# Pinning ScalarE's first operation for the w_in pieces only in an attention + FFN + MoE kernel

## The chip, the cores and the metric

One NeuronCore of a Trainium2 chip runs the whole program in one launch. The metric is the device time of that launch in microseconds, as the median of several runs; lower is better. The profile is one further execution with the hardware profiler on.

## The reference, cut to what matters

```python
def reference(q, k, v, M_prev, z_prev, beta, moe_w_in, moe_w_out, w_gate, w1, w2):
    # attention: 4 batches x 8 heads, 576 tokens, 64 wide, causal softmax plus a gated memory read
    x = (g * mem_out + (1 - g) * local)            # -> [2304, 512]
    # dense feed-forward: 512 -> 2048 -> 512
    h = x @ w_in
    x = np.maximum(h, 0.0) ** 2 @ w_out
    # mixture: 8 experts of capacity 288, tokens dealt out in order of their logits
    return moe2(x, w_gate, w1, w2)                 # [2304, 512], float32
```

`w_in` and `w_out` arrive as 64-bit floats and are narrowed to 32 bits on the chip; what else matters here is float32. The change touches how these two weights are made ready.

## The kernel before, in words

**Stages.** The program runs attention for 16 pairs of heads, then the dense feed-forward in three passes over the 2048 hidden columns, then the mixture. The stages overlap: while attention runs, the first pass of the feed-forward (hidden chunks 0 to 5 of 16, `PASSES[0]`) is already prepared and, from the fifth head pair on, computed between attention's matmuls. A step of attention (`step(n)`, n from -2 to 16) works on three or four head pairs at once; its ten sub-steps follow `PLAN` and call `fill` 20 times with a count of feed-forward matmuls that may go in there.

**Weight pieces.** Matmuls run on pairs of a rounded high part and a remainder, so each weight is split first. A piece is 128 partitions by 512 values of 64 bits. The first pass has twelve: pieces 0 to 5 are chunks of `w_in` (part 0), pieces 6 to 11 chunks of `w_out` (part 1). The generator `apart` makes them in this order, and `fill` advances it by one piece at places given in `CONVERT`: two per step in steps 0 to 5 (at the 10th and 20th call of `fill`; in step 5 at the 4th and 10th). So the w_out pieces belong to steps 3, 4 and 5. One piece costs:

- `fetch` (L424): one DMA of 512 KB from SyncE's queue into tile `raw`. There are two such tiles in turn, and the fetch stands in the program one piece ahead of its use. SyncE's queue is in order, and the fetch of piece n+2 waits until piece n has been read by L39.
- `narrow`: L36 on ScalarE (`r<-raw`), then L37, L38 and L39 on VectorE (`gf<-r`, `r<-r,gf`, `gf<-raw,r`).
- `split`: L25 on ScalarE (`win<-gf` or `wout<-gf`) and L26 on GpSimd (`wout<-gf,wout`).

**What sets the order.** TensorE's order is the program's, written by hand (`INORDER`). For the other engines the build plays the program on its own model of times and gives each engine's queue the order that comes out; on the chip each queue then runs strictly in that order, and an instruction whose input is late holds up all behind it. `keep_in_program_order(a)` ties an instruction to come behind the instruction that precedes it on its engine in the program. In `weights` it ties L36 of every first-pass piece (`first` is true when the pool is `f.start`), in `fetch` the DMA of every first-pass piece. For pieces 6, 8 and 11 the preceding ScalarE instruction is the eviction L316 of the first-range read (`read(n, 0, ..)`); for pieces 7 and 9 it is the end of a step; for piece 10 it is the exponential L173 of `phi`. The 20 pieces of the two later passes (`chunks`, pools `cv`) have no such tie.

**Names used below.** L217 scores, L228 and L236 their masking on VectorE, L240 exponentials on ScalarE, L246 scaling on GpSimd, L271 and L287 transposes on TensorE, L25/L26 the high part and remainder of any split, L312 the read of the values, L316 its eviction, L162 the remainder of the values (`vt`), L172 to L185 `phi` (tile `e` has one buffer: L172 of one head pair waits for L180 of the pair before), L474 the sum of two halves of a token block (`xf`), L487 the ReLU that empties the hidden accumulator `ph`.

Of the kernel before, what the change touches and what calls it, by code (L numbers as in the profile page):

```python
# [22 lines left out]
def split(nc, hi, lo, src, eng=None):  # L23

    a = nc.scalar.activation(hi, src, AF.Copy)  # L25
    (eng or nc.vector).tensor_tensor(lo, src, hi.bitcast(F32), op=OP.subtract)  # L26
    return a.ins


def narrow(nc, f, tmp, raw):  # L30

    low, high = raw[..., 0], raw[..., 1]
    a = nc.scalar.activation(tmp.bitcast(F32), high.bitcast(F32), AF.Copy, scale=2.0 ** -112)  # L36
    nc.vector.tensor_scalar(f, tmp, 3, None, op0=OP.logical_shift_left)  # L37
    nc.vector.scalar_tensor_tensor(tmp, tmp, -2 ** 31, f, op0=OP.bitwise_and, op1=OP.bitwise_or)  # L38
    nc.vector.scalar_tensor_tensor(f, low, 29, tmp, op0=OP.logical_shift_right, op1=OP.bitwise_or)  # L39
    return a  # L40
# [353 lines left out]
class Ffn:  # L394
# [34 lines left out]
    def weights(self, c, part, home, pool, eng, psum=None, raw=None):  # L429

        nc = self.nc
        if part == 0:
            a = self.win[c] = home.tile([128, 2, KD, 128], F32R, name="win")
            dst = a.rearrange("p s k f -> p s (k f)")
        else:
            dst = self.wout[c] = home.tile([128, 2, DM], F32R, name="wout")
        first = pool is self.start
        raw = self.fetch(c, part, pool) if raw is None else raw
        t_ = (psum or self.two).tile([128, DM], I32, name="pr" if psum and psum is self.p2x else "r")
        held = part and c >= PASSES[-1][0]  # L440
        f_ = (self.two if first else self.keep if held else pool).tile([128, DM], I32, name="gf")
        a = narrow(nc, f_, t_, raw.rearrange("p (n t) -> p n t", t=2))
        if first:
            self.tc.keep_in_program_order(a)
        split(nc, dst[:, 0], dst[:, 1], f_.bitcast(F32), eng)
        if held:
            self.sums += [(f_, c - PASSES[-1][0], e) for e in range(8)]
        yield
# [846 lines left out]
```

## Time and profile before

| what | before |
|---|---|
| median of 3 runs | 1045.69 us (1044.23 to 1046.37) |
| the profiled execution | 1049.03 us, its span 1047.3 us |
| TensorE busy | 959.4 us (92%) |
| VectorE, ScalarE, GpSimd busy | 655.2, 552.6, 540.3 us |

How to read it: the profiled execution lies 3.34 us above the median of the runs, and its span 1.73 us below its own time. Engines are PE (TensorE), PEld (its weight loads), DVE (VectorE), ACT (ScalarE), POOL (GpSimd) and SP (SyncE); a "q" behind the name is the engine's sequencer. "Idle before" is the time that an engine stood ahead of an instruction, with what ended it.

### The profile page before, as it was taken

To read this page: it belongs to the slowest core of one execution; us is meant where nothing else is said; L and a number is where in the kernel's file an instruction comes from. 1 tells how busy PE (TensorE), PEld (TensorE's weight loads), DVE (VectorE), ACT (ScalarE), POOL (GpSimd) and SP (SyncE) were. 2 spreads that over 40 slices of the span, in tenths; PEclk is the share of its full clock that TensorE was granted. 3 is DMA by queue.
4 is the path that set the end of the run, shared out by engine and by line. 5 is a ranking of instruction groups with operands and counts; after the bars stand their busy time and mean duration, and the time that the engine had idled before them with its cause. 6 is when DMAs were issued, how large, how long until landed. Compare 5 with 4: busy or idle time off the path is not lost.

```text
span 1047.3 us, 19732 instructions
## 1 busy us (share of the span) xinstructions
PE 959.4 (92%) x7017; PEld 879.1 (84%) x7017; DVE 655.2 (63%) x1925; ACT 552.6 (53%) x1370; POOL 540.3 (52%) x535
## 2 busy tenths in 40 slices
PE   5777879999999988999999999999598999999996
PEld 3666668988889987999999999877498888989996
DVE  6889888888888737256427943335775567674110
ACT  6778878888888735444322343431252453344531
POOL 4666776766666525344312121211394865687841
PEclk9778889999999999999999999999698999999999
DMA  6345736374526277769583332101542444437400
GB/s 154 106 123 142 192 89 179 75 196 100 172 67 175 56 233 227 220 223 315 185 293 122 117 125 83 68 12 41 193 162 79 152 184 151 156 130 258 147 28 27
DMA packets 150724, 150.75 MB, mean 144 GB/s; under 512 B 71641, under 2 KB 122841, under 8 KB 150497
## 3 DMA queue, kind: packets, MB, share of 16 engines
q1 hardware_dynamic: 147552, 140.05, 43.6%
q0 software_dynamic: 3072, 9.44, 2.9%
q8 instruction: 55, 0.90, 0.4%
q14 instruction: 45, 0.36, 0.1%
HBM read 111.69 MB, written 37.77 MB: 143 GB/s over the span
## 4 chain that ended last, share of the span: by engine, by line
PE 61%; DVE 12%; issue 7%; DMA 6%; ACT 6%; POOL 5%; SPq 1%; POOLq 0%; DVEq 0%; ACTq 0%
PE ph L1066 12%; PE ph L45 6%; PE ph L46 6%; PE ph L47 6%; PE py L45 4%; PE py L46 4%; PE py L47 4%; PE ps L312 3%; POOL wsp L1050 3%; PE ps L217 3%; PE ps L271 2%; PE rs L843 2%; DMA raw<-in_moe_w_out_dram 1%; DMA raw<-in_moe_w_in_dram 1%; ACT P L240 1%
## 5 line engine op out<-in xcount | busy, mean ns | idle before, releaser
L489 POOL TENSOR_TENSOR gf<-r 128x384 f32<-128x384 f32 (+1 forms) x108 | 87.4, 810 | 206.9 <-ACT r L487 198.1
L1050 POOL TENSOR_TENSOR wsp<-wraw,wsp 128x1024 fp32r<-128x1024 f32 x64 | 150.9, 2393 | 42.8 <-ACT wsp L1048 31.6
L26 DVE TENSOR_TENSOR gs<-gf,gs 128x384 fp32r<-128x384 f32 (+1 forms) x108 | 65.6, 607 | 91.4 <-ACT gs L25 90.9
L1066 PE MATMUL ph<-xs,wsp 128*128 128x288 f32 x768 | 120.0, 306 | 0.0
L1066 PE MATMUL ph<-hs,wsp 128*128 128x288 f32 x768 | 117.5, 307 | 0.0
L246 POOL TENSOR_SCALAR P<-P,R,og 128x128 f32<-128x128 f32 (+2 forms) x144 | 99.5, 707 | 24.6 <-DVE R L244 17.7
L1066 PEld LDWEIGHTS ph<-xs,wsp 128*128 128x128 f32 x768 | 106.6, 192 | 3.6 <-issue 2.8
L1066 PEld LDWEIGHTS ph<-hs,wsp 128*128 128x128 f32 x768 | 107.2, 194 | 0.9 <-DVE hs L1090 0.4
L1048 ACT ACTIVATE wsp<-wraw 128x1024 fp32r<-128x1024 f32 x64 | 64.0, 1051 | 48.6 <-DMA wraw<-in_moe_w_dram 29.1
L487 ACT ACTIVATE r<-ph 128x384 f32<-128x384 f32 (+1 forms) x108 | 48.6, 450 | 77.6 <-PE ph L47 76.5
L240 ACT ACTIVATE P<-P,R 128x128 f32<-128x128 f32 (+2 forms) x144 | 83.4, 580 | 8.4 <-DVE R L228 6.9
L25 ACT ACTIVATE gs<-gf 128x384 fp32r<-128x384 f32 (+1 forms) x108 | 52.5, 486 | 58.0 <-POOL gf L489 49.6
L45 PE MATMUL ph<-xt,win 128*128 128x384 f32 x240 | 81.3, 339 | 0.0
L46 PE MATMUL ph<-xt,win 128*128 128x384 f32 x240 | 80.8, 337 | 0.0
L47 PE MATMUL ph<-xt,win 128*128 128x384 f32 x240 | 80.7, 336 | 0.0
L45 PE MATMUL ph<-xs,win 128*128 128x288 f32 x192 | 64.3, 335 | 10.6 <-ACT r L487 7.6
L271 PE MATMUL ps<-ident,P 128*128 128x128 f32 x320 | 62.3, 302 | 8.6 <-DVE R L228 3.3
L46 PE MATMUL py<-gs,wout 128*128 128x384 f32 x192 | 64.7, 338 | 0.3 <-DVE gs L26 0.3
L47 PE MATMUL py<-gs,wout 128*128 128x384 f32 x192 | 63.9, 336 | 0.0
L26 DVE TENSOR_TENSOR ptb<-ps,ptb 128x384 fp32r<-128x384 f32 (+3 forms) x128 | 59.1, 464 | 7.4 <-ACT ptb L25 5.8
L45 PE MATMUL py<-gs,wout 128*128 128x384 f32 x192 | 63.4, 338 | 0.0
L228 DVE CUSTOM_DVE_ANT_0 P<-ps,maskw 128x128 f32<-128x128 f32 (+3 forms) x128 | 58.5, 483 | 6.2 <-PE ps L217 3.2
(259 smaller groups left out, 2596.4 us busy)
## 6 DMA issues: line engine op xcount, KB each, us to landing
wraw<-in_moe_w_dram SPq DMA_DIRECT2D x32, 1024.0 KB, 5.5
xt<-xs_d SPq DMA_DIRECT2D x12, 1536.0 KB, 7.2
x_d<-xo SPq DMA_DIRECT2D x32, 288.0 KB, 3.8
xf<-x_d SPq DMA_DIRECT2D x32, 288.0 KB, 3.8
xs_d<-xs SPq DMA_DIRECT2D x8, 1152.0 KB, 6.6
raw<-in_moe_w_in_dram SPq DMA_DIRECT2D x16, 512.0 KB, 5.4
raw<-in_moe_w_out_dram SPq DMA_DIRECT2D x16, 512.0 KB, 5.5
yp<-yo SPq DMA_DIRECT2D x32, 144.0 KB, 3.9
```

The lines of the kernel that those rows point to most:

```text
L26: (eng or nc.vector).tensor_tensor(lo, src, hi.bitcast(F32), op=OP.subtract)
L45: nc.tensor.matmul(out, lhi, rhi, start=start, stop=False)
L46: nc.tensor.matmul(out, lhi, rlo, start=False, stop=False)
L47: nc.tensor.matmul(out, llo, rhi, start=False, stop=stop)
L228: nc.vector.tensor_tensor_reduce(out=pw, in0=ps[:, 0:W[u]], in1=maskw[:, 512 - 128 * t:640], op0=OP.add, op1=OP.min, scale=-0.125, scalar= ...
L240: nc.scalar.activation(pw, pw, AF.Exp, bias=R[:, 0, u:u + 1], scale=-1.0, accum_out=R[:, 1, u:u + 1])
L246: nc.gpsimd.tensor_scalar(PP[n][w], PP[n][w], R[:, 2, w:w + 1], og9[:, hp, w:w + 1], op0=OP.mult, op1=OP.mult)
L271: nc.tensor.transpose(tr[:, 128 * i:128 * i + 128], P[:, 128 * i:128 * i + 128], ident)
L489: nc.gpsimd.tensor_tensor(gf, r, r, op=OP.mult)
L1048: nc.scalar.activation(w[:, 0, hs], raw[:, hs], AF.Copy)
L1050: eng.tensor_tensor(w[:, 1, hs], raw[:, hs], w[:, 0, hs].bitcast(F32), op=OP.subtract)
L1066: nc.tensor.matmul(out, l[a], r[b], start=i + p == 0, stop=i == n - 1 and p == 2)
```

## The change

In `weights`, L36 is tied to its place only for pieces with `part` 0, those of `w_in`. For the six pieces of `w_out` the tie is gone, and the build places L36 on ScalarE as it places any other instruction. The tie of the fetches, the places in `CONVERT`, the tiles, and all instructions and their number stay.

```diff
         a = narrow(nc, f_, t_, raw.rearrange("p (n t) -> p n t", t=2))
-        if first:
+        if first and not part:
             self.tc.keep_in_program_order(a)
         split(nc, dst[:, 0], dst[:, 1], f_.bitcast(F32), eng)
```

## Rows read from the trace of the kernel before

**Rows 1.** The page: the span.

```profile
span 1047.3 us, 19732 instructions
```

**Rows 2.** Stretches: us, busy (count) of PE, PEld, DVE, ACT, POOL; clock, DMA, GB/s.

```profile
75.50:96.20 20.70, 16.54 (x101) 13.20 (x100) 20.26 (x60) 17.55 (x52) 13.85 (x15) 0.83 0.58 151
96.20:118.30 22.10, 16.79 (x102) 13.32 (x101) 20.55 (x58) 17.73 (x53) 16.21 (x20) 0.81 0.60 159
118.30:139.00 20.70, 17.98 (x122) 14.73 (x121) 17.30 (x52) 16.41 (x50) 17.04 (x21) 0.94 0.55 149
139.00:148.40 9.40, 3.42 (x17) 3.41 (x18) 6.55 (x15) 5.57 (x12) 7.62 (x10) 0.64 0.63 158
...
191.00:350.00 159.00, 156.57 (x1188) 140.99 (x1187) 133.72 (x405) 134.88 (x410) 104.70 (x136) 1.00 0.48 126
```

**Rows 3.** Line L36, whole span: min/median/max ns, first and last start; idle before.

```profile
L36 ACT ACTIVATE r<-raw x20: 624/660/685, 30.1 to 417.9; 128x512 f32<-128x512 f32 x20
L36 ACT ACTIVATE pr<-raw x12: 607/638/652, 448.0 to 501.4; 128x512 f32<-128x512 f32 x12
...
  DMA raw<-in_moe_w_in_dram: 11.7, 7
  DMA raw<-in_moe_w_out_dram: 7.6, 6
```

**Rows 4.** Line L36, 0 to 160 us (no idle time before it there).

```profile
L36 ACT ACTIVATE r<-raw x12: 645/662/685, 30.1 to 149.2; 128x512 f32<-128x512 f32 x12
```

**Rows 5.** ScalarE in order: start, us, line, operation, [idle before <-what ended it].

```profile
96.24 0.39 ACT L316 ACTIVATE xo<-ps 128x256 f32<-128x256 f32 x1 [1.17 <-PE ps L312]
...
118.30 0.39 ACT L316 ACTIVATE xo<-ps 128x256 f32<-128x256 f32 x1 [1.92 <-PE ps L312]
118.58 0.66 ACT L36 ACTIVATE r<-raw 128x512 f32<-128x512 f32 x1
...
142.44 0.74 ACT L172 ACTIVATE e<-nq 128x640 f32<-128x640 f32 x1 [2.24 <-DVE nr L180]
...
143.84 0.65 ACT L36 ACTIVATE r<-raw 128x512 f32<-128x512 f32 x1
144.51 0.41 ACT L487 ACTIVATE r<-ph 128x288 f32<-128x288 f32 x1
```

**Rows 6.** VectorE in order, around three of the six pieces.

```profile
97.21 0.86 DVE L37 TENSOR_SCALAR gf<-r 128x512 int32<-128x512 int32 x1 [0.62 <-ACT r L36]
...
119.27 0.84 DVE L37 TENSOR_SCALAR gf<-r 128x512 int32<-128x512 int32 x1 [1.36 <-ACT r L36]
...
130.74 0.79 DVE L37 TENSOR_SCALAR gf<-r 128x512 int32<-128x512 int32 x1
131.44 0.40 DVE L26 TENSOR_TENSOR ptb<-ps,ptb 128x256 fp32r<-128x256 f32 x1
```

**Rows 7.** TensorE in order: a wait in step 4, one in step 5, the first use of w_out.

```profile
131.90 0.55 PE L217 MATMUL ps<-kt,qt 64*128 64x128 f32 x6 [1.01 <-DVE ptb L26]
...
144.98 0.61 PE L45 MATMUL ph<-xs,win 128*128 128x288 f32 x1 [6.65 <-ACT r L487]
...
157.75 0.38 PE L45 MATMUL ph<-gs,wout 128*128 128x288 f32 x1
```

**Rows 8.** Lines L37, L38, L39 from 96 to 155 us, the six w_out pieces.

```profile
L37 DVE TENSOR_SCALAR gf<-r x6: 387/606/858, 97.2 to 150.1; 128x512 int32<-128x512 int32 x6
...
L38 DVE SCALAR_TENSOR_TENSOR r<-r,gf x6: 674/693/1279, 99.4 to 150.9; 128x512 int32<-128x512 int32 x6
...
L39 DVE SCALAR_TENSOR_TENSOR gf<-raw,r x6: 677/788/1112, 102.6 to 152.8; 128x512 int32<-128x512 int32 x6
```

**Rows 9.** Fetches: SyncE's issue for piece 8; landing of the six w_out fetches.

```profile
103.57 0.35 SPq L424 DMA_DIRECT2D raw<-in_moe_w_out_dram  x1
...
DMA to landing us min/median/max: 3.7/4.0/6.3
```

**Rows 10.** GpSimd beside the longest L38, that of piece 8, issued at 120.50.

```profile
120.43 0.80 POOL L474 TENSOR_TENSOR xf<-xf 128x288 f32<-128x288 f32 x1 [0.24 <-DMA xf<-x_d]
```

## The prediction, made before the changed kernel was run

> **What bounds the kernel now.** I read the table of stretches first. From 191 to 350 us TensorE is busy 156.57 of 159 us at full clock [rows 2]: there it is the bound, its order is fixed by hand and its work is not touched. What the change can give or take must come before that, in steps 3 to 5 of attention, where the six w_out pieces are made. Step 3 has VectorE busy 20.26 of 20.70 us and 20.55 of 22.10 us in the two stretches that hold it; in step 4 it is at 17.30 of 20.70; between 139.0 and 148.4 us nothing is busy for long, TensorE 3.42 of 9.40 us at a clock of 0.64 [rows 2]. So the bound moves: VectorE first, then a chain of waits, then TensorE. A microsecond won before about 148 us arrives at the end nearly whole, since TensorE is full from there on.
>
> Second, the lists of instructions in order of time, around each L36. ScalarE stands 1.17 and 1.92 us ahead of the eviction L316 and then runs L316 and L36 back to back: 118.30 plus 0.39, next 118.58 [rows 5]. The tie binds, then: L36 goes at the first moment that it may. Third, who waited for it: VectorE stood 0.62 us (piece 6) and 1.36 us (piece 8) until L36 was done [rows 6]. In step 4 TensorE stood 1.01 us for a remainder (L26) that was queued behind piece 9's L37 [rows 6, 7]. In step 5 TensorE stood 6.65 us for the ReLU L487, which started at 144.51 us right behind piece 10's L36 at 143.84 [rows 5, 7].
>
> **The change part by part.** No instruction is added or dropped. What moves is six L36 and, behind them, six each of L37, L38, L39, L25 and the GpSimd L26. They can only go earlier, as the tie was a lower bound. How much earlier is set by the data: piece 8's fetch is issued at 103.57 us and such a fetch lands 3.7 to 6.3 us later, 4.0 in the median [rows 9], so its L36 could go from about 107.6 us, 11 us ahead of 118.58 [rows 5]. The fetches stay tied on SyncE, but each waits for L39 two pieces before, so an earlier L39 lets a fetch go earlier too; that is no cost, since SyncE holds less behind it.
>
> Piece 6. If L36 sits in the 1.17 us ahead of L316 [rows 5], L37 can use the 0.62 us that VectorE stood [rows 6]: a gain of 0.62 us, at most the 0.86 us of L37 itself. VectorE is full on both sides [rows 2], so what it gains counts.
>
> Piece 8. Likewise 1.36 us [rows 6], with room for L36 in 1.92 us [rows 5]. Bounds: nothing, if the operations land in VectorE's full stretch before; up to 2.78 us, the sum of L36 (0.66), L37 (0.84) and L38 (1.28, the longest of its row), if all three leave the path [rows 5, 6, 8]. I take 1.36, the row that shows an engine standing.
>
> Piece 9. L37 (0.79 us) stands ahead of the L26 for which TensorE waits 1.01 us [rows 6, 7]. Gain 0.79, between nothing and 1.01.
>
> Piece 10. L36 leaves the queue between L173 and L487: 144.51 minus 143.84, 0.67 us off the wait of 6.65 [rows 5, 7].
>
> Pieces 7 and 11: nothing. No wait of an engine is shown behind their L36 in steps 3 and 5, and the first use of any w_out tile is at 157.75 us [rows 7]; the last piece's L39 starts at 152.8 at the latest [rows 8].
>
> Sum of gains: 0.62 + 1.36 + 0.79 + 0.67 = 3.44 us.
>
> Costs. Every freed L36 takes 0.66 us of ScalarE at its new place [rows 4]. For pieces 6, 8 and 10 a gap that could take it is in the rows, 1.17, 1.92 and 2.24 us [rows 5]; for piece 9 I know none, and charge 0.66 us. Bounds: 0 and four times 0.66, 2.6 us. GpSimd's subtraction moves with its piece; GpSimd is busy 16.21 and 17.04 us of steps of 22.1 and 20.7 [rows 2], and I charge nothing: if that cover is gone, a due operation of the read waits behind it.
>
> Expected gain: 3.44 - 0.66 = 2.78 us. On the profiled span of 1047.3 [rows 1] that gives 1044.5; its execution lies 3.34 us above the median of the runs, so I take the gain off the median: 1045.69 - 2.78 = **1042.9 us**.
>
> **A rule against it.** Piece 8's L38 took 1.28 us where the shortest took 0.674, and it was issued at 120.50 while a GpSimd addition ran from 120.43 for 0.80 us [rows 8, 10]: it ended 0.55 us after that addition did. The Trainium skill (page "SBUF — State Buffer", section "Who interferes with whom") says that a VectorE operation with two inputs in SBUF and a GpSimd operation that reads SBUF exclude each other, the second waiting until the first is done. The row agrees with it. So where the 18 moved operations land beside GpSimd decides their length. Now they take about 6 x (0.606 + 0.693 + 0.788) = 12.5 us by their medians; at the shortest it is 10.4, at the longest 6 x (0.858 + 1.279 + 1.112) = 19.5 [rows 8]. That is -2.1 to +7.0 us of VectorE work, and it is a rival below.
>
> **The rivals.**
>
> 1. *Slower: ScalarE parks at a freed L36.* The order is made on a model of times; on the chip the fetch may land later than the model has it, and all of ScalarE's queue then stands. The kernel shows it: of the 20 pieces of the later passes, which have no tie, 13 had ScalarE standing for the fetch, 19.3 us in all, 1.48 each [rows 3]; of the twelve tied ones none [rows 4]. At that rate 3.9 of 6 park, 5.8 us. The gains of pieces 6 and 8 are lost with it, those of 9 and 10 (1.46) stay: +4.3 us, **1050.0**. It decides from three parked pieces on (3 x 1.48 is more than 3.44). For it: without the tie L36 may go as soon as the model has the fetch landed, and the model need not be right by 4 us [rows 9]. Against it: ScalarE is busy 17.6 of 20.7 us here [rows 2], the freed operation comes last among those ready, and the fetch stands one piece ahead. 0.22.
>
> 2. *Nothing: VectorE is full.* The moved operations only push others in a stretch that is already 93 to 98% busy [rows 2], and the idle times come back elsewhere. Then 0.7 us at most remains, from piece 10: **1045.3**. 0.22.
>
> 3. *The stall in step 5 goes.* L487 waits behind L172, which waits 2.24 us for L180 [rows 5]. If the new order has L487 ahead of L172, or brings L180 forward by what pieces 8 to 10 leave on VectorE, up to 6.65 - 0.67 = 6.0 us more go: **1036.9**, or about 1040 for half. The order of the two is set by the model and not by the tie, so this is a by-product. 0.10.
>
> 4. *Slower by the port:* the moved operations meet GpSimd's long run of L246 at their longest, +7.0 - 2.78: **1049.9**. Six of six at the longest is unlikely. 0.05.
>
> 5. *It doesn't do what it says:* something else (the fetch, a tile) keeps each L36 where it is: **1045.7**. The leads of about 11 us speak against it. 0.03.
>
> **How the numbers follow.** The forecast itself has 0.38, with a range of its own of 1041.5 to 1044.5. What a measurement of this kernel can tell from no change is about 0.2%, 2.1 us. Faster by more: 0.32 of the forecast's 0.38 and rival 3, 0.42. Within: the other 0.06 less a little, rivals 2 and 5, 0.30. Slower by more: rivals 1 and 4, and the unnamed small part, 0.28. The range leaves out the far half of rival 3 and about half of rivals 1 and 4: 1038 to 1050.
>
> **What would show it.** Right: in the trace after, L36 of pieces 6 and 8 ahead of L316, in its idle time; no idle time of VectorE that ends with L36; L26 ahead of piece 9's L37 and a shorter wait of L217; L487 right behind L173; the stretch 191 to 350 unchanged but about 2.8 us earlier. Wrong: idle time of ScalarE ahead of L36 that a fetch ends (rival 1), the steps as long as before with VectorE's idle time elsewhere (rival 2), a wait of TensorE in step 5 far from 6 us (rival 3), L37 to L39 all near 0.9 to 1.3 us (rival 4). A wait of several microseconds at a new place, where a queue in order meets an operation that the model had earlier, would make the whole sum wrong.

## The result: slower by half a per cent to one per cent

| | before | after |
|---|---|---|
| median | 1046.37 us (1044.23 to 1049.26, 5 runs) | 1052.84 us (1051.41 to 1053.47, 5 runs) |
| ratio after to before | | 1.0053, 95% interval 1.0032 to 1.0074 |
| the same on a second chip | 1055.81 us (17 runs) | 1066.11 us (6 runs), ratio 1.0098, 1.0064 to 1.0132 |
| profiled execution, its span | 1049.03, 1047.3 us | 1051.83, 1050.1 us |

The forecast was 1042.9 us, faster. The time lies outside its range and on the other side.

To compare traces I cut them at the same instructions. TensorE's order is the same in both kernels, so the first transposes L131 of `nk` of successive head pairs (start 73.46, 93.35, 114.66 and, three marks on, 190.54 us before) bound three stretches of the same TensorE work: the **first** stretch (piece 6 lands in it when freed), the **second** (from about 93 us) and the **third** (three head pairs, with the 6.65 us wait for L487). From there on both kernels do the same.

The kernel before was profiled a second time beside the experiments. Here are its stretches two and three (the third in two rows), then those of the changed kernel. Columns are as in [rows 2].

```profile
94.52:115.98 21.46, 16.57 (x100) 12.99 (x100) 20.21 (x58) 18.09 (x54) 15.51 (x18) 0.83 0.60 156
115.98:148.67 32.69, 23.09 (x142) 19.53 (x143) 26.80 (x72) 22.53 (x62) 27.35 (x32) 0.81 0.64 172
148.67:194.00 45.33, 43.63 (x319) 39.20 (x319) 36.55 (x104) 36.21 (x110) 25.91 (x33) 0.95 0.48 126
```

```profile
93.40:123.40 30.00, 23.67 (x100) 18.70 (x100) 21.97 (x58) 18.68 (x53) 20.27 (x22) 0.55 0.49 127
123.40:145.70 22.30, 20.60 (x142) 17.79 (x143) 20.98 (x59) 18.29 (x54) 14.43 (x19) 0.92 0.53 136
145.70:197.00 51.30, 45.40 (x320) 40.03 (x318) 39.41 (x115) 39.27 (x116) 32.78 (x41) 0.93 0.53 140
197.00:356.00 159.00, 156.64 (x1188) 141.13 (x1187) 133.47 (x405) 134.58 (x408) 104.97 (x137) 1.00 0.48 126
```

The second stretch grew from 21.5 to 30.0 us. The same 100 matmuls were busy 23.67 instead of 16.57 us at a granted clock of 0.55 instead of 0.83. GpSimd did 22 operations instead of 18. The third stretch shrank from 78.0 to 73.7 us. Behind it the row of 159 us is that of [rows 2], 156.64 us busy against 156.57. So most of the loss is the second stretch, less a part of it won back in the third; the first is 1 to 3 us longer (table below).

What happens at its start, in the changed kernel: ScalarE's four L36 (pieces 6, 7, 8, and 11), then VectorE, GpSimd and TensorE in order of time (start, us, operation, idle before).

```profile
86.08 0.69 ACT L36 ACTIVATE r<-raw 128x512 f32<-128x512 f32 x1
92.11 0.73 ACT L36 ACTIVATE r<-raw 128x512 f32<-128x512 f32 x1
96.27 0.67 ACT L36 ACTIVATE r<-raw 128x512 f32<-128x512 f32 x1 [0.83 <-DMA raw<-in_moe_w_out_dram]
...
150.31 0.69 ACT L36 ACTIVATE r<-raw 128x512 f32<-128x512 f32 x1 [1.77 <-DMA raw<-in_moe_w_out_dram]
```

```profile
95.81 1.75 DVE L37 TENSOR_SCALAR gf<-r 128x512 int32<-128x512 int32 x1 [1.37 <-POOL win L26]
97.60 0.69 DVE L200 TENSOR_TENSOR qpt<-ps,qpt 64x512 fp32r<-64x512 f32 x1
...
115.35 0.29 DVE L228 CUSTOM_DVE_ANT_0 P<-ps,maskw 128x128 f32<-128x128 f32 x1 [1.71 <-PE ps L217]
...
120.58 0.42 DVE L228 CUSTOM_DVE_ANT_0 P<-ps,maskw 128x256 f32<-128x256 f32 x1 [3.93 <-PE ps L135]
```

```profile
94.51 1.27 POOL L26 TENSOR_TENSOR win<-gf,win 128x512 fp32r<-128x512 f32 x1
95.74 1.54 POOL L177 TENSOR_TENSOR e<-qp,zb 128x640 f32<-128x640 f32 x1
```

```profile
98.34 1.33 PE L217 MATMUL ps<-kt,qt 64*128 64x384 f32 x6 [1.96 <-DVE qpt L200]
...
101.92 2.52 PE L217 MATMUL ps<-kt,qt 64*128 64x512 f32 x6
...
115.68 2.17 PE L312 MATMUL ps<-ptb,vt 128*128 128x320 f32 x8
...
190.07 0.39 PE L304 MATMUL ps<-qpt,mb 128*128 128x320 f32 x1 [2.46 <-DVE ptb L26]
```

Pieces 6, 7 and 8, which stood 11 us apart, now come within 10 us. Piece 7's L37 writes one of two tiles `gf`; piece 5's subtraction on GpSimd (94.51 plus 1.27) still reads the one it needs, so L37 waits 1.37 us. It then takes 1.75 us, where the longest of before took 0.86 [rows 8], beside L177 on GpSimd. L200, whose end frees the PSUM bank that the scores L217 write, is queued behind it, and TensorE stands 1.96 us. The same two instructions in the second profile of the kernel before:

```profile
101.13 1.29 PE L217 MATMUL ps<-kt,qt 64*128 64x512 f32 x6
...
109.69 1.25 PE L312 MATMUL ps<-ptb,vt 128*128 128x320 f32 x8
```

Behind the wait the changed kernel's matmuls take nearly twice as long up to about 120 us: 2.52 against 1.29, 2.17 against 1.25. There the roles turn: VectorE stands 1.71 and 3.93 us for L217 and L135; before, its waits for TensorE in this stretch come to 0.2 us.

### The profile page after: what moved, and what is told of

Same layout as the page of the kernel before. It is cut to its first block, busy times and chain, and to the rows that moved or that the text cites. A ratio compares the mean times of both kernels' runs of the same rounds, so it can differ in the third digit from the quotient of the medians.

```text
span 1050.1 us, 19731 instructions
## 1 busy us (share of the span) xinstructions
PE 967.3 (92%) x7017; PEld 885.2 (84%) x7017; DVE 654.7 (62%) x1925; ACT 553.8 (53%) x1370; POOL 540.7 (51%) x535
## 4 chain that ended last, share of the span: by engine, by line
PE 63%; DVE 11%; issue 7%; DMA 6%; POOL 5%; ACT 5%; SPq 2%; POOLq 0%; DVEq 0%; ACTq 0%
PE ph L1066 12%; PE ph L45 7%; PE ph L46 6%; PE ph L47 6%; PE py L45 4%; PE py L46 4%; PE py L47 4%; PE ps L312 3%; PE ps L217 3%; POOL wsp L1050 3%; PE rs L843 2%; PE ps L271 2%; DMA xf<-x_d 2%; PE ps L131 1%; DVE ptb L26 1%
## 5 line engine op out<-in xcount | busy, mean ns | idle before, releaser
L26 DVE TENSOR_TENSOR gs<-gf,gs 128x384 fp32r<-128x384 f32 (+1 forms) x108 | 67.4, 624 | 92.7 <-ACT gs L25 92.3
L487 ACT ACTIVATE r<-ph 128x384 f32<-128x384 f32 (+1 forms) x108 | 48.6, 450 | 78.0 <-PE ph L47 76.8
L45 PE MATMUL ph<-xt,win 128*128 128x384 f32 x240 | 81.4, 339 | 0.0
L45 PE MATMUL ph<-xs,win 128*128 128x288 f32 x192 | 64.1, 334 | 3.8 <-ACT yo L526 2.5
L26 DVE TENSOR_TENSOR ptb<-ps,ptb 64x64 fp32r<-64x64 f32 (+3 forms) x128 | 59.1, 463 | 8.0 <-ACT ptb L25 6.4
L45 PE MATMUL py<-gs,wout 128*128 128x384 f32 x192 | 63.4, 338 | 0.0
```

The costliest lines, as they stand in the source:

```text
L45: nc.tensor.matmul(out, lhi, rhi, start=start, stop=False)
```

## The experiments

All kernels of a set ran on one chip, beside the kernel before on that chip. The edits are to the kernel before, where nothing else is said; c counts from 0 for piece 6 to 5 for piece 11. One table for all; lengths of the three stretches in us, from one profile each, and the second's granted clock where I read it:

| kernel | L36 free | first | second (clock) | third | ratio, 95% interval |
|---|---|---|---|---|---|
| before | none | 19.9 | 21.3 (0.82) | 75.9 | |
| before_again | none | 19.9 | 21.5 (0.83) | 78.0 | 1.0004, 0.9977 to 1.0031 |
| after | 6 to 11 | 22.8 | 30.0 (0.55) | 73.7 | 1.0053, 1.0032 to 1.0074 |
| after_again | 6 to 11 | 21.0 | 30.4 (0.56) | 73.1 | 1.0098, 1.0064 to 1.0132 |
| free678 | 6, 7, 8 | 22.3 | 29.7 (0.62) | 72.9 | 1.0067, 1.0036 to 1.0098 |
| free6_7 | 6, 7 | 20.9 | 26.7 (0.69) | 74.9 | 1.0050, 1.0022 to 1.0078 |
| free6 | 6 | 20.9 | 20.0 (0.84) | 76.7 | 1.0020, 0.9994 to 1.0046 |
| free7 | 7 | 19.9 | 22.4 | 77.0 | 1.0025, 1.0003 to 1.0047 |
| free8 | 8 | 22.4 | 22.5 | 77.1 | 1.0039, 1.0015 to 1.0062 |
| free9_11 | 9, 10, 11 | 20.5 | 20.6 | 73.0 | 0.9953, 0.9927 to 0.9980 |
| free10 | 10 | 19.9 | 20.7 (0.92) | 72.9 | 0.9943, 0.9918 to 0.9968 |
| free10_again | 10 | 19.9 | 21.7 (0.84) | 73.0 | 0.9978, 0.9956 to 1.0000 |
| not7 | all but 7 | 21.2 | 21.8 (0.81) | 77.8 | 1.0043, 1.0019 to 1.0067 |
| not6 | all but 6 | 19.9 | 24.6 (0.79) | 74.4 | 1.0034, 1.0007 to 1.0061 |
| slow200 | none | 19.9 | 26.9 (0.83) | 76.9 | 1.0083, 1.0055 to 1.0110 |
| after_busy | 6 to 11 | 20.9 | 25.8 (0.68) | 71.5 | 1.0015, 0.9989 to 1.0041 |
| before_busy | none | 19.9 | 21.4 (0.84) | 78.0 | 1.0006, 0.9984 to 1.0029 |
| free10_busy | 10 | 19.9 | 23.1 (0.85) | 75.3 | 0.9990, 0.9966 to 1.0014 |
| after_gw | 6 to 11 | 20.9 | 26.9 (0.63) | 75.0 | 1.0018, 0.9995 to 1.0040 |
| before_gw | none | 19.9 | 20.7 (0.92) | 77.2 | 1.0049, 1.0030 to 1.0067 |

Two profiles of one kernel (before, after, free10) agree within 1.0 us in the second stretch and 2.1 in the third. In the first, single profiles are off by 2 us: the 22.4 of free8 lie ahead of anything that its edit moves. Behind the third stretch, where all kernels do the same, the profiled executions last 851 to 867 us, up to 7 us apart on one chip. So a profile's total shows none of these effects; the ratios are of medians.

**Halves of the change.** The first question was which pieces carry the loss.

```diff
-        if first:
+        if first and not (part and c < 3):      # free678
+        if first and not (part and c > 2):      # free9_11
+        if first and not (part and c == 4):     # free10
```

> Only pieces 6, 7 and 8 lose the tie, 9 to 11 keep it. In the changed kernel these three run their L36 at 86.1, 92.1 and 96.3 us, all within step 3. Theory A (three pieces crowd VectorE's queue in step 3, where it is full; L37 of piece 7 stands for a gf buffer and the clock falls behind it): the step that holds 93 to 123 us stays near 30 us as against 21.3 before, and since piece 10 keeps its tie the wait of TensorE for L487 in step 5 stays too, so 5 to 10 us over the kernel before. Theory B (ScalarE parks at L36 for its fetch): 0.83 us of parking is all there is in these three, so at most 1 us slower.

> Only pieces 9, 10 and 11 lose the tie, 6 to 8 keep it. Theory A: steps 3 is as in the kernel before, the 6.65 us wait of TensorE for L487 in step 5 goes or shrinks below 2 us, so 3 to 7 us faster than the kernel before. Theory B: parking at L36 of piece 11 (1.77 us in the changed kernel) makes it 0 to 2 us slower. Theory C (what hurts is the step after, 146 to 174 us, 28.5 us in the changed kernel as against 21.2 before, and pieces 9 to 11 cause it): 3 to 7 us slower.

> Only piece 10 loses the tie. Theory A: the wait of TensorE for L487 in step 5 (6.65 us before) goes or falls below 2 us because L487 no longer stands behind L172, L173 and L36; 3 to 6 us faster than the kernel before. If the wait is made by L172 alone: 0.7 us faster, the wait about 6 us.

Pieces 6 to 8 alone give the loss, 1.0067, with the long second stretch. Pieces 9 to 11, and 10 alone, make the kernel faster: the wait of L45 for L487 is gone from the list of TensorE's waits in the third stretch of free10, which now begins (line, waited for: us in all, times, longest):

```profile
PE ps L312 <- POOL vt L162: 1.7, 1, 1.7
PE ps L131 <- issue: 1.5, 1, 1.5
PE ps L271 <- POOL gf L489: 1.4, 1, 1.4
```

On ScalarE L487 now stands ahead of L172, where it stood behind it [rows 5]:

```profile
140.53 0.41 ACT L487 ACTIVATE r<-ph 128x288 f32<-128x288 f32 x1
...
144.98 0.73 ACT L172 ACTIVATE e<-nq 128x640 f32<-128x640 f32 x1
```

Of the 6.65 us that wait cost, that stretch became 3.0 to 5.1 us shorter (72.9 against 75.9 and 78.0); the time gained is 2.3 us (0.22% on one chip) to 6.0 us (0.57% on another). free678 shows the other side of it: its wait for L487 is 7.43 us, longer than before, and its third stretch is 72.9 us too, so this wait and the length of the stretch don't go one to one.

**Which of 6, 7 and 8.**

```diff
+        if first and not (part and c == 0):     # free6 (free7: c == 1, free8: c == 2)
+        if first and not (part and c < 2):      # free6_7
```

> The tie is taken from L36 of piece 6 alone. Theory A (crowding: the loss needs piece 7 close behind piece 6 in step 3, where its L37 waits for one of two gf tiles and L200 stands behind it): L36 of piece 6 starts at about 86 us as in the changed kernel, piece 7 stays near 107 us, TensorE doesn't wait about 2 us for L200 near 98 us, the step behind it stays near 21 us, and the ratio to the kernel before is within 0.998 to 1.002. Rival B (the loss comes from piece 6 being early at all, because its three VectorE operations land in a full stretch): the step is 25 us or longer and the ratio is 1.003 or more.

> The tie is taken from L36 of piece 7 alone; piece 6 stays behind L316 at about 96 us and piece 7 goes right behind it. Theory A: nothing is crowded into 86 to 97 us, so the step from 93 us keeps its 21 us; pieces 6 and 7 now share the time from 97 to 105 us, and the second L37 waits for a gf tile there, at most about 1.5 us: ratio 0.998 to 1.004. Rival B (each freed early piece costs about a third of the 0.67% of the three together): 1.002.

> The tie is taken from L36 of piece 8 alone; it goes right behind piece 7 at the end of step 3, so that VectorE's idle 1.36 us ahead of its L37 can go, as the prediction had it. Theory A: 0.996 to 1.000, a gain of up to 1.4 us, the step from 93 us unchanged. Rival B: 1.002.

> The ties of pieces 6 and 7 are taken. Theory A: the crowding is back with these two: L36 at about 86 and 92 us, L37 of piece 7 waits more than 1 us for GpSimd's subtraction, TensorE waits about 2 us for L200 near 98 us at a granted clock well below 0.8 in the step from 93 us, which takes 26 to 30 us; ratio 1.003 to 1.008, nearly all of the loss of the three together. Rival B: two thirds of 0.67%, 1.0045, but without the wait for gf. Rival C (it takes all three, since the fetch of piece 8 and its parking are needed): 0.998 to 1.002.

The second stretch bears out theory A: it is 20.0 to 22.5 us with one piece free and 26.7 with 6 and 7, where VectorE's and TensorE's rows repeat those of the changed kernel:

```profile
98.67 1.74 DVE L37 TENSOR_SCALAR gf<-r 128x512 int32<-128x512 int32 x1 [2.20 <-POOL win L26]
100.45 0.69 DVE L200 TENSOR_TENSOR qpt<-ps,qpt 64x512 fp32r<-64x512 f32 x1
```

```profile
101.19 1.33 PE L217 MATMUL ps<-kt,qt 64*128 64x384 f32 x6 [1.96 <-DVE qpt L200]
```

No idle time of ScalarE ahead of an L36 ends with a fetch in free6_7, so the loss needs no parking. But the times don't bear theory A out alone: the single pieces cost 0.20, 0.25 and 0.39%, which for 7 and 8 is what rival B had, though their second stretch is not long. The interval of piece 6 includes 1 and that of piece 7 begins at 1.0003; for piece 8 a loss is left that I can't place. Its profile can't show it: that execution took 1046.68 us, the shortest of its twelve, with a median of 1051.23. Rival B is not excluded.

**One tie put back.** Both start from the changed kernel.

```diff
-        if first and not part:
+        if first and (not part or c == 1):      # not7 (not6: c == 0)
```

> The changed kernel with the tie put back for piece 7 alone; 6 and 8 to 11 stay free. If the crowding of pieces 6 and 7 on VectorE and its two gf tiles is the cause: piece 7 at about 107 us or later, no wait of L217 for L200 near 98 us, the step from 93 us at 20 to 23 us with a granted clock of 0.8 or more, and with the gain of pieces 9 to 11 kept, a ratio of 0.992 to 0.998. If the loss belongs to any early piece: 1.002 or more.

> The changed kernel with the tie put back for piece 6 alone; 7 to 11 stay free. Pieces 6 and 7 now stand back to back behind L316, at about 97 us. If the crowding has to meet the L200 of the second head (at 95 to 98 us) to hurt: no such wait, the step at 21 to 24 us, ratio 0.994 to 1.000. If two early pieces in this step are enough wherever they stand: step 26 us or more, ratio 1.003 or more.

With piece 7 tied the second stretch is 21.8 us again and L217 doesn't wait for L200: both have to be early for that. With piece 6 tied it is 24.6, between my two expectations. But the ratios stay above 1, against what theory A expected: in not7 the third stretch is 77.8 us, so the gain of pieces 9 to 11 isn't there. The crowding of 6 and 7 accounts for the long second stretch and not for all of the time; what not7 and not6 lose stays open. In the third stretch GpSimd's L474 waits longer for its load (`xf`) than before; first not7, then the changed kernel (123.4 to 197 us), then before_again:

```profile
POOL xf L474 <- DMA xf<-x_d: 8.7, 2, 6.7
```

```profile
POOL xf L474 <- DMA xf<-x_d: 17.8, 4, 7.6
```

```profile
POOL xf L474 <- DMA xf<-x_d: 4.5, 2, 4.3
```

In the changed kernel the longest of them ends at 188.34, and TensorE's longest wait of the stretch, 2.46 us at 190.07, comes behind it, though what ended that wait was VectorE's L26. The load was issued at 184.76, behind loads of q and k and stores in SyncE's queue, where before_again has the fourth such load ahead of them (171.53). One of those, and the load:

```profile
182.35 1.05 SPq L78 DMA_DIRECT2D nk<-in_k_dram  x2
...
184.76 0.60 SPq L473 DMA_DIRECT2D xf<-x_d  x1
```

How much of the third stretch this costs was not measured by itself.

**The wait and the clock.** The 30 us hold a wait of 2 us and matmuls that are 7.1 us longer. Is the clock the price, or the held queue? slow200 adds VectorE work to the kernel before; after_busy and before_busy repeat three transposes ahead of the waiting L217, into the same place, so that TensorE works there instead of standing.

```diff
-                nc.vector.tensor_tensor(q_[o, c0:c1], src, q_[a, c0:c1].bitcast(F32), op=OP.subtract)
+                [nc.vector.tensor_tensor(q_[o, c0:c1], src, q_[a, c0:c1].bitcast(F32), op=OP.subtract) for _ in range(5 if n == 3 and part == 0 and j == 1 else 1)]
```

```diff
-                for i in range(t + 1):
+                for i in [i for _ in range(3 if n == 3 and step == 5 else 1) for i in range(t + 1)]:
                     nc.tensor.transpose(tr[:, 128 * i:128 * i + 128], P[:, 128 * i:128 * i + 128], ident)
```

> The kernel before with all ties, and the disputed cost alone: the subtraction L200 of the second head of pair 3 (at 95.0 us in the trace of the kernel before, 0.69 us) is issued five times instead of once, with the same inputs and result, so that the scores L217 behind it (at 96.79 us) wait about 2 us, as they do in the changed kernel. Theory A1 (a stall of this size in step 3 lets the granted clock fall, and the longer matmuls are most of the loss): the granted clock of the step from 93 us goes from 0.82 to 0.65 or less, the step goes from 21.3 us to 26 us or more, ratio 1.003 to 1.006. Rival A2 (a stall costs what it lasts; the loss comes from the three pieces' work itself): the step takes 23 to 24.5 us, clock about 0.8, ratio 1.001 to 1.0025.

> The changed kernel with the three transposes L271 that stand ahead of the waiting scores L217 (at 95.5 us) issued three times, into the same place, so that TensorE works in the 1.96 us in which it stood. If the granted clock that follows the wait is most of the loss: clock of the step at 0.75 or more, L217 of 64x512 near 1.0 us instead of 2.52, step of 24 us or less instead of 30, ratio 0.998 to 1.003. If the held VectorE queue is the loss by itself: step of 27 us or more whatever the clock, ratio 1.005 to 1.010.

> The kernel before, all ties in place, with the three transposes L271 ahead of L217 (at 96.0 us there) issued three times. TensorE doesn't wait at that place in this kernel. If what helped the changed kernel was the filled wait: no gain here, step from 93 us 21 to 23.5 us (six transposes of 0.15 to 0.3 us each in a step that VectorE fills), ratio 0.999 to 1.003. If six more transposes there help in any case: 0.997 or less.

> The kernel with the tie taken from piece 10 alone, which gave 0.9943 and 0.9978, with the same six transposes. If the filled wait is what matters: no further gain, 0.995 to 1.000. If the transposes help in any case: below 0.994.

slow200 fits neither theory: its length is A1's, its mean clock A2's, and its time lies above both. The build spread the five L200 from 95.57 to 107.77 us, so the scores didn't wait; another matmul did, for the last of them. The stretch took 26.9 us with TensorE's busy time and mean clock unchanged:

```profile
93.90:120.80 26.90, 16.70 (x100) 13.53 (x101) 22.87 (x62) 18.80 (x52) 18.55 (x22) 0.83 0.50 136
```

```profile
108.52 0.58 PE L304 MATMUL ps<-qpt,mb 128*128 128x256 f32 x1 [2.84 <-DVE qpt L200]
```

So 4 x 0.69 = 2.8 us of VectorE work in this stretch cost 5.4 us of it (26.9 against 21.5), and 8.8 us of the kernel (0.83%), with no longer matmuls in sum. In this run the added work cost twice its length in the stretch; that other work does so is not shown. The other 3.4 us are not explained.

The equal mean hides that the low level of the clock moved. Here are parts of the second stretch in before_again, slow200, the changed kernel and after_busy; the granted clock is the third number from the end, 0.50 is 1.2 GHz and 1.00 is 2.4 GHz:

```profile
96.00:101.00 5.00, 4.74 (x21) 3.77 (x21) 4.32 (x11) 2.06 (x5) 3.23 (x4) 0.50 0.79 185
102.00:113.00 11.00, 9.03 (x64) 7.14 (x60) 10.56 (x36) 10.88 (x35) 7.82 (x10) 1.00 0.39 105
```

```profile
98.00:104.00 6.00, 3.44 (x21) 2.08 (x19) 5.84 (x13) 4.25 (x9) 0.84 (x3) 1.00 0.58 141
106.00:111.00 5.00, 2.48 (x11) 2.48 (x12) 3.94 (x15) 3.23 (x10) 2.91 (x3) 0.50 0.54 164
112.00:118.00 6.00, 4.25 (x36) 3.54 (x34) 3.75 (x11) 3.97 (x13) 6.00 (x7) 1.00 0.28 90
```

```profile
94.00:98.00 4.00, 2.38 (x11) 1.76 (x9) 2.60 (x3) 2.70 (x6) 4.00 (x4) 0.50 1.07 263
98.00:119.00 21.00, 18.10 (x71) 14.44 (x72) 16.08 (x46) 11.70 (x36) 12.91 (x17) 0.50 0.36 96
```

```profile
94.00:110.00 16.00, 13.38 (x54) 10.61 (x54) 13.58 (x30) 9.11 (x22) 11.54 (x13) 0.50 0.64 151
112.00:119.00 7.00, 5.35 (x42) 4.35 (x40) 4.99 (x20) 6.83 (x26) 5.66 (x8) 1.00 0.51 130
```

In slow200 the low level lies about its wait of 2.84 us and not ahead of it, and is about as long as before. In the changed kernel the clock was low already when the wait of 1.96 us began (96.38), as it was at this place in before_again. What differs is that it stayed low until about 120 us, across that wait and four shorter ones (0.26 to 0.99 us). In free678 the clock was high through a wait of 2.26 us at this place and low behind it for as long; in free6_7, with the wait of 1.96 us, it was low for a shorter time and in two parts. So the wait alone doesn't fix how long it is low:

```profile
97.00:99.00 2.00, 0.00 (x0) 0.00 (x0) 1.95 (x2) 1.15 (x3) 2.00 (x2) 1.00 1.22 219
101.00:119.00 18.00, 15.86 (x62) 12.72 (x61) 14.28 (x42) 11.21 (x35) 11.89 (x15) 0.50 0.31 89
```

```profile
95.00:104.00 9.00, 5.59 (x25) 4.37 (x25) 6.58 (x11) 3.61 (x9) 7.07 (x7) 0.50 0.81 210
105.00:111.00 6.00, 4.12 (x25) 2.70 (x24) 6.00 (x21) 5.46 (x16) 5.16 (x7) 1.00 0.27 87
112.00:118.00 6.00, 6.00 (x29) 5.66 (x28) 2.93 (x14) 3.93 (x15) 4.45 (x7) 0.50 0.23 57
```

after_busy has the same wait for `gf` as after_again (2.20 and 2.19 us) and 1.3 us more of matmuls (2.14 us for nine transposes against 0.86 for three), and its second stretch is shorter: 25.8 instead of 30.0 and 30.4. Its ratio, 1.0015, lies below 1.0053 and 1.0098, but the two kernels didn't run beside each other on one chip, and its interval overlaps that of the first.

```profile
94.35:120.13 25.78, 20.73 (x105) 16.76 (x106) 21.32 (x58) 18.69 (x55) 18.91 (x21) 0.68 0.61 148
```

```profile
97.33 2.14 PE L271 MATMUL ps<-ident,P 128*128 128x128 f32 x9
100.16 1.33 PE L217 MATMUL ps<-kt,qt 64*128 64x384 f32 x6 [0.69 <-DVE qpt L200]
```

The same six transposes do nothing for the kernel before (1.0006, 21.4 us) and nothing more for free10 (0.9990). So the transposes help only where TensorE stood: some 4 of the 9 us that the second stretch grew by hang on that, with the low level ending near 111 us and not near 120 (mean 0.68 against 0.55). The rest, some 4, I put on VectorE's held queue, which is argued and not shown: the queue is held for the 1.37 us ahead of L37 and for the 1.3 us by which L37 is longer than the 0.42 us that the next one took, 2.7 us together, as much as the work added in slow200. The build also moved some operations on the other engines behind the six transposes, so the split is rough.

**The two tiles.** after_gw gives every second w_out piece a third tile for `gf` (and stores the mask tile at half width to make room); before_gw is the same in the kernel before.

```diff
-        f_ = (self.two if first else self.keep if held else pool).tile([128, DM], I32, name="gf")
+        f_ = (pool if first and part and c % 2 else self.two if first else self.keep if held else pool).tile([128, DM], I32, name="gw" if first and part and c % 2 else "gf")
```

> The changed kernel, with a tile gw of its own for the words of w_out's odd pieces (7, 9, 11) in place of the two gf tiles that all share; the room comes from storing the mask of the last block at half its width, the other half being zeros that maskw holds too. L37 of piece 7 no longer waits for GpSimd to release gf. Theory A with the buffer as its cause: the 1.37 us of idle time ahead of piece 7's L37 and the long L37 (1.75 us) go, the step from 93 us is 3 us or more shorter than 30 us, total 2 to 5 us faster than the changed kernel. If crowding alone matters and not the buffer: within 2 us of the changed kernel.

> The kernel before, all ties in place, with the third gf tile (gw) for every second w_out piece and the halved mask tile: a control for the run with the third tile in the changed kernel, which gave 1.0018. If the third tile by itself brings nothing: 0.999 to 1.001, and what it took off the changed kernel's loss is the wait for gf. If it brings 0.3% here too, that run says nothing on the wait.

In after_gw the wait of L37 for `gf` is gone and L217 waits 0.9 us for L200 instead of 2.0, yet the stretch still takes 26.9 us at 0.63, and L37 still 1.30 us. So the wait for the tile is worth about 3 of the 9 us, which overlaps with the 4 above; the rest is not the tile. The profile is that of the slowest of its twelve executions (1066.65 us, median 1058.37). Its time, 1.0018, says less: the control lost 0.49% though its three stretches are those of before, so the edit has an effect elsewhere that I didn't trace. That the third tile is worth anything in time stays open.

**The changed kernel and free10 again**, on one chip:

> The changed kernel once more, unchanged, beside the others on one chip: 1.0053, within 1.0032 to 1.0074, if the first measurement holds; in the profile again two or three L36 between 86 and 97 us, a wait of about 2 us of L217 for L200 near 98 us, and a step from 93 us of 26 to 30 us at a granted clock below 0.7. If the step's length came from that one execution's clock and not from the order, the step is 21 to 23 us here.

> The tie is taken from L36 of piece 10 alone, once more and on the same chip as the changed kernel: 0.9943, within 0.9918 to 0.9968, if that measurement holds. The wait of L45 for L487 of 6.65 us is gone in the profile, and the two steps from 147 us on take about 45 us instead of 43.

> The kernel before, once more, with a profile of its own: a ratio of 1.000 within its interval, and the steps from 93 us and from 114 us within 1 us of the 21.3 and 32.7 us read first, if one profile can stand for a kernel there; if these differ by 3 us or more, the steps of single profiles can't carry a cause.

The long second stretch and the 1.97 us wait of L217 are there again in after_again. Both ratios miss what I expected from the first measurement: 1.0098 lies above 1.0032 to 1.0074, 0.9978 above 0.9918 to 0.9968. Of six freed L36, three had ScalarE standing for a fetch (0.19, 1.92 and 2.22 us). free10 measured faster on both chips, clearly on the first; on the second its interval ends at 1.0000. It is the version to take, 0.2 to 0.6% ahead of the kernel before, and 1.2% ahead of the changed one where both ran on one chip (0.9978 against 1.0098).

## Why the prediction was wrong, step by step

**"Pieces 7 and 11: nothing"** is the step that failed, in its term for piece 7. I priced the pieces one by one, each at the row where it stood before, and for piece 7 saw no wait behind it. But one tie held all that follows: with piece 6 early, its L39 releases the fetch of piece 8 earlier, piece 7 has no bound of its own, and the three come together at 86 to 97 us. The range that I gave piece 8 (from 107.6 us) was already wrong: its L36 starts at 96.27. Pieces 6 and 7 together add 5.3 us to the second stretch (free6_7), with piece 8 it is 8.2 to 8.9; with piece 7 tied again it is nearly gone (21.8 us, not7), though a loss of time is left.

**GpSimd "charged nothing"** failed with it. I named a due operation of the read as what would wait; it was the tile `gf`, which the next piece's L37 can't write before GpSimd's subtraction has read it. GpSimd's busy time in the stretch went from 15.51 to 20.27 us.

**Pieces 6 and 8** (0.62 and 1.36 us of VectorE's idle time). Freed alone, piece 6 moves three VectorE operations from one full stretch to another: the first grew by 1.0 us (19.9 to 20.9), the second shrank by 1.3 to 1.5, and the third and the time show no gain (1.0020). Piece 8 alone: no gain either (1.0039). The idle times were real; what filled them pushed others, which is what my second rival said.

**Piece 9** (0.79 us): the wait of L217 for L26 in step 4 is not among the waits of half a microsecond or more in the changed kernel's third stretch. Within the 2 us by which that stretch varies, its worth can't be told.

**Piece 10** (0.67 us) was mis-sized, downward. I took off the length of one L36; the whole wait of 6.65 us went, as my third rival had it, because the order of L487 and L172 changed too. But of the 6.65 us at most 6.0 reached the time. In the changed kernel the next two steps are longer instead: 51.3 against 43.1 and 45.3 us, and VectorE has 115 operations in them where it had 104. While TensorE stood, the other engines had caught up.

**SyncE: "no cost, since SyncE holds less behind it".** Not shown: GpSimd stood 17.8 us for loads of `xf` in the third stretch, where it had stood 4.5. The longest of these loads stands behind loads of q and k and not behind a fetch of a piece, so what moved it, and what it costs in time, stay open.

**The clock** had no place in the sum. I read 0.81 and 0.83 in the very stretches [rows 2] and took the matmuls' lengths as fixed there. Of the 8.5 us by which the second stretch grew, 7.1 are longer matmuls.

**The rival that came in was none of mine.** Rival 1 came near the time with 1050.0, for the wrong reason: ScalarE parked for 2.6 us in all (two of six) in the changed kernel, where I charged 5.8, and free6_7 loses as much without any parking. Rival 2's 1045.3 doesn't follow from its words: 0.7 us off 1045.69 gives 1045.0. Rival 4 was half there: piece 7's L37 took 1.75 us beside GpSimd's L177 and ended 0.28 us after it, but VectorE's busy time for the same 58 operations rose by 1.8 us only, of the 7.0 that I gave as an end. The Trainium skill (page "SBUF — State Buffer", section "Who interferes with whom") says that a `tensor_scalar`, which has one input, can in its two-port modes also take the port pair that VectorE shares with GpSimd, and that the one issued first keeps it for its whole instruction. The row agrees roughly (L177 was issued 0.07 us ahead, and 0.28 us are left behind its end where an L37 took 0.42); that L37 ran in such a mode is not shown. I had looked only at operations with two inputs, and there too the fit was rough: the 0.55 us left to piece 8's L38 are less than the 0.674 of the shortest. What did come was in the prediction's last sentence: a wait at a new place, where a queue in order meets an operation that the model had earlier.

**Left open:** what the single pieces 7 and 8 lose, why not7 and not6 lose, how the second stretch's growth divides between the held queue and the clock, the control's 0.49%, and why the changed kernel loses twice as much on the second chip. One profile a kernel can't show a difference of 2 us there.

## What to carry to other kernels

A tie in a chain of pieces holds all pieces behind it, through its tiles and fetches; before you price freeing it, lay out where the whole chain can then go, and look for the fullest queue that it can reach. Price each tile of two by who reads it last, on whatever engine that is. A wait that you remove is worth what the other engines didn't need it for: here a wait of 6.65 us was worth 2 to 6. And read the clock in short parts of a stretch: two equal means, 0.83, had their low level in different places.

## What the runs showed of the hardware that I had not expected

The granted clock stayed at its lower level for 25 us in which TensorE worked most of the time: 0.50 (1.2 GHz) from 94 to 119 us in the changed kernel, with 6 x 512 columns in 2.52 us instead of 1.29. In before_again the level was low just ahead too (0.50 from 96 to 101 us) and 1.00 (2.4 GHz) from 102 us. With the wait filled by 1.3 us of useless transposes the level rose near 111 us, and that stretch took 25.8 us instead of 30. The Trainium skill (page "TensorE: Matmul & The Clock Gate", section "Loop structure matters more than you think") says that a loop with long waits between its matmuls leaves TensorE at its lower clock. The runs agree in part: the low part of before_again stands behind waits of 1.45 and 0.90 us, that of slow200 (0.50 from 106 to 111 us) about its wait of 2.84 us. But the wait of 1.96 us alone doesn't say how long the level stays low: free6_7 has the same wait and is at 1.00 from 105 us, to fall again by 112. What decides it is open.
